# Output rows staged in eight row buffers, and one half block sent from the ACT queue

## The chip, the core and the metric

The kernel runs on one core of a Trainium2 chip. A core has five engines that run their own instruction streams: TensorE (PE, matrix products into PSUM), VectorE (DVE), ScalarE (ACT), GpSimd (POOL) and SyncE (SP, which here issues all DMA transfers). They are kept in order by semaphores: an instruction can wait until a counter has reached a value, and can raise one when it is done; a DMA raises its counter when its data has landed. The metric is the device time of one execution in microseconds, lower being better.

## The reference, cut to what matters

```python
x = A_x                                              # (1, 2048, 512) bf16
h = x + _A_ref(_layernorm(x, axis=-1), A_mem0, A_Wq, A_Wk, A_Wv, A_Wo, A_seg_len)
h2 = h + _B_ref(_layernorm(h, axis=-1), B_w_in, B_w_sp, B_b_sp, B_w_out)

def _B_ref(x, w_in, w_sp, b_sp, w_out):
    Fh = w_in.shape[-1] // 2                         # 896
    z = _gelu(jnp.einsum('bsd,df->bsf', x, w_in))
    z1 = z[..., :Fh].copy()
    z2 = _layernorm(z[..., Fh:], axis=-1)
    g = jnp.einsum('ts,bsf->btf', w_sp, z2) + b_sp[None, :, None]
    return jnp.einsum('bsf,fd->bsd', z1 * g, w_out)
```

`_A_ref` is an attention with 32 heads over 64 segments of 32 rows, one after the other, since each hands 8 memory rows to the next. `_B_ref` is a gated mixer over all 2048 rows. The change touches the last step of all: the product `(z1 * g) @ w_out`, the addition of `h`, and the way of the result to memory.

## The kernel before, in words

The 2048 rows are held as 16 row blocks of 128 rows, one row per partition. The first stage runs the 64 segments; it ends near 688 us. In it `part` (line 232) is a ring of eight row buffers of 128 x 512 values: the ACT engine writes segment s's attention output into buffer `s % 8` (`part_evac`, line 671), and PE reads it in `mem_out` (line 675) and `F_group` (line 692). The last of these reads belongs to row block 15 and is made at the start of the second stage. `xn` (line 234) is a pair of row buffers for normalised input.

The second stage computes `z2` and `z1T`, then, in four blocks `tb` of 512 rows, the mixing product (`mix`, line 1091: 16 matmuls per group) and its gate on DVE (`gate`, line 1096: two DVE instructions). As rows become complete, `out_mm` (line 1164) multiplies a row block with `w_out` (7 matmuls into one PSUM bank), and `out_done` (line 1170) adds `h` from `h_sb` on DVE into a row buffer and lets SP issue the DMA to the output. The first 12 output blocks are spread between the mixing groups of the following `tb`. The last four are written out by hand in lines 1202 to 1212: the first six matmuls of blocks 12 and 13, then, after the last gate, the seventh matmul of each with its `out_done`; then block 14 whole; then block 15 as two halves of 256 columns, in banks 5 and 7.

The instruction order of each engine is the order in which the program adds operations. The waits are worked out from tokens: `Emitter.add` (line 53) makes an operation wait for the last writer of each token that it reads, and for the last writer and all readers of each token that it writes; `finalize` (line 110) drops a wait that an earlier one of the same engine implies. The DMA out of a row buffer is a reader of that buffer's token. With two buffers, `xn[:, rb % 2]`, the addition of block rb therefore waits until the DMA of block rb - 2 has landed:

```python
tok = [("xo_out", rb % 2, hf) for hf in range(2) if d0 <= 256 * hf < d1]
dve(... out=xn[:, rb % 2, d0:d1] ..., writes=tok + [("xn", rb % 2)] * (rb < 2))
sp(lambda e: e.dma_start(outr[:, rb, d0:d1], xn[:, rb % 2, d0:d1]), reads=tok)
```

After its own stream each engine runs `run` (line 1893): it loads a flag from memory (line 1896; the flag says whether a slower general path is needed), and branches over that path (line 1900) to the end of the block (line 1905), where it drains and reports. SP first waits for the landing of the last DMA of every one of its DMA semaphores (line 1899). When all have reported, GpSimd releases them, and the program ends. ACT and GpSimd have no work in the last output blocks: they wait for the flag (line 1215), written at 795.8 us, and go to the end then.

Of the kernel before, what the change touches and what calls it, by code (L numbers as in the profile page):

```python
# [10 lines left out]
ALU = mybir.AluOpType  # L11
# [158 lines left out]
def fast_path(nc, st, keep, A_x, A_mem0, A_Wq, A_Wk, A_Wv, A_Wo, A_seg_len, B_w_in, B_w_sp, B_b_sp, B_w_out, out):  # L170
    S = A_x.shape[1]
    D = A_x.shape[2]
# [6 lines left out]
    RB = S // 128  # L179
# [16 lines left out]
    em = Emitter(n_dma_sems=40)  # L196

    def sb(name, shape, dt):
        return st.enter_context(nc.sbuf_tensor("f_" + name, shape, dt))
# [5 lines left out]
    def region(off, n):  # L205
        return arena[:, off:off + n]
# [25 lines left out]
    part = sb("part", [128, 8, 512], BF)  # L232
    partx = sb("partx", [128, 512], BF)
    xn = sb("xn", [128, 2, 512], BF)
# [28 lines left out]
    ps = st.enter_context(nc.psum_tensor("f_ps", [128, 8, 512], F32))  # L263
# [5 lines left out]
    def PB(b):  # L269
        return ("ps", b)  # L270

    def sp(fn, **k):
        return em.add("sp", fn, dma=True, **k)
# [15 lines left out]
    def dve(fn, **k):  # L289
        return em.add("dve", fn, **k)  # L290
# [552 lines left out]
    h_sb = region(RB * 512, RB * D).rearrange("p (rb d) -> p rb d", rb=RB)  # L843
# [14 lines left out]
    for s in range(NSEG):  # L858
        j4 = s % 4
        rb = s // 4  # L860
# [244 lines left out]
    def zbank():  # L1105
        zcnt[0] += 1
        return 5 + zcnt[0] % 3
# [5 lines left out]
    for rb in range(RB):  # L1113
# [19 lines left out]
        if rb in (2, 3):  # L1133
            r, j, bank = RB - 4 + rb, (rb - 1) % 2, zbank()
# [27 lines left out]
    outr = out[0].rearrange("(rb p) d -> p rb d", p=128)  # L1162

    def out_mm(rb, fbs, bank, d0=0, d1=D):
        for fb in fbs:
            pe(lambda e, fb=fb: e.matmul(ps[:, bank, 0:d1 - d0], lhsT=z1T[:, fb, rb * 128:(rb + 1) * 128], rhs=w_out[:, fb, d0:d1],  # L1166
                                         start=(fb == 0), stop=(fb == FB - 1)),
               reads=["w_out", ("z1T", fb, rb // 4)], writes=[PB(bank)])

    def out_done(rb, bank, d0=0, d1=D):  # L1170
        tok = [("xo_out", rb % 2, hf) for hf in range(2) if d0 <= 256 * hf < d1]
        dve(lambda e: e.tensor_tensor(out=xn[:, rb % 2, d0:d1], in0=ps[:, bank, 0:d1 - d0], in1=h_sb[:, rb, d0:d1], op=ALU.add),
            reads=[PB(bank), ("hs", rb)], writes=tok + [("xn", rb % 2)] * (rb < 2))
        sp(lambda e: e.dma_start(outr[:, rb, d0:d1], xn[:, rb % 2, d0:d1]), reads=tok)

    def out_rb(rb):
        bank = 2 + rb % 2
        out_mm(rb, range(FB), bank)
        out_done(rb, bank)
# [4 lines left out]
    for tb in range(NTB):  # L1184
        for fb in range(len(ACC) if tb == 0 else 0, FB):
            if tb == 0:
                bank = 5 + fb % 3
            else:
                bank = MB[mcnt % 3]
# [14 lines left out]
    for rb in pend[:2]:  # L1204
        out_mm(rb, (FB - 1,), 2 + rb % 2)
        out_done(rb, 2 + rb % 2)
    out_mm(RB - 2, range(FB), 6)
    out_done(RB - 2, 6)
    for d0 in (0, 256):
        bank = 7 if d0 else 5  # L1210
        out_mm(RB - 1, range(FB), bank, d0, d0 + 256)
        out_done(RB - 1, bank, d0, d0 + 256)

    for eng in Emitter.ENGS:
        em.add(eng, None, reads=["flag"])
# [668 lines left out]
def build_kernel(nc, A_x, A_mem0, A_Wq, A_Wk, A_Wv, A_Wo, A_seg_len, B_x, B_w_in, B_w_sp, B_b_sp, B_w_out, out):  # L1884
    args = (A_x, A_mem0, A_Wq, A_Wk, A_Wv, A_Wo, A_seg_len, B_w_in, B_w_sp, B_b_sp, B_w_out, out)
    with contextlib.ExitStack() as keep:
        with contextlib.ExitStack() as st:
            em, sems, dsems, flag = fast_path(nc, st, keep, *args)
# [88 lines left out]
```

The softmax here doesn't subtract the row's maximum and nothing guards it: scores larger than these inputs give would overflow.

## Time and profile before

| | |
|---|---|
| time, median of 6 runs | 870.91 us (869.59 to 871.8) |
| time of the profiled execution | 870.33 us |
| its span, first to last instruction | 868.5 us |
| PE busy | 847.5 us, 98% of the span |
| DVE / ACT / POOL busy | 502.0 / 467.0 / 157.9 us |
| granted TensorE clock, mean | 0.997 |
| last matmul starts | 860.66 us |
| output DMAs (line 1174) | 15 of 128 KB, 2 of 64 KB, all from SP |

The page splits the span by engine in 40 slices of 21.7 us, follows the chain of work that ended last, and groups instructions by line. A time line shows instructions in order with the idle time before them in brackets and what ended it. Lines that begin with an engine and a "q" (DVEq, SPq) belong to the engine's sequencer: waits, branches, loads of a flag, DMA issues. The duration of a DMA issue is the time that the issuing queue spends on it, not the time of the transfer; the landing is marked apart, by the semaphore that the DMA raises. The difference between the profiled execution's time and its span, 1.8 us, lies around the first and the last instruction.

### The profile page before, as it was taken

To read this page: it belongs to the slowest core of one execution; us is meant where nothing else is said; L and a number is where in the kernel's file an instruction comes from. 1 tells how busy PE (TensorE), PEld (TensorE's weight loads), DVE (VectorE), ACT (ScalarE), POOL (GpSimd) and SP (SyncE) were. 2 spreads that over 40 slices of the span, in tenths; PEclk is the share of its full clock that TensorE was granted. 3 is DMA by queue.
4 is the path that set the end of the run, shared out by engine and by line. 5 is a ranking of instruction groups with operands and counts; after the bars stand their busy time and mean duration, and the time that the engine had idled before them with its cause. 6 is when DMAs were issued, how large, how long until landed. Compare 5 with 4: busy or idle time off the path is not lost.

```text
span 868.5 us, 45456 instructions
## 1 busy us (share of the span) xinstructions
PE 847.5 (98%) x22453; PEld 432.3 (50%) x18876; DVE 502.0 (58%) x1246; ACT 467.0 (54%) x1291; POOL 157.9 (18%) x427
## 2 busy tenths in 40 slices
PE   6999999999999999999999999999999999999996
PEld 6664545544545444554444544545444444444443
DVE  3446666666666666666666666566565554454343
ACT  3445666666666666666666666666666655300000
POOL 1712112121122112121212112121111122100000
PEclk9999999999999999999999999999999999999998
DMA  9972332213141232222250313322221880033001
GB/s 320 380 221 70 71 70 74 65 39 84 33 86 40 68 64 30 73 68 63 67 97 26 83 51 81 80 70 71 47 68 43 197 267 1 0 109 111 25 19 33
DMA packets 114183, 75.23 MB, mean 87 GB/s; under 512 B 70712, under 2 KB 99520, under 8 KB 113984
## 3 DMA queue, kind: packets, MB, share of 16 engines
q1 hardware_dynamic: 113984, 72.26, 30.5%
q8 instruction: 164, 2.69, 1.3%
q14 instruction: 35, 0.29, 0.1%
HBM read 39.46 MB, written 20.58 MB: 69 GB/s over the span
## 4 chain that ended last, share of the span: by engine, by line
PE 96%; DVE 2%; DMA 1%; issue 1%; ACT 0%; POOL 0%; SPq 0%; DVEq 0%
PE f_ps L280 30%; PE f_ps L660 13%; PE f_ps L281 13%; PE f_ps L1092 11%; PE f_ps L710 3%; PE f_ps L426 3%; PE f_ps L461 3%; PE f_ps L1054 3%; PE f_ps L574 3%; PE f_ps L1085 3%; PE f_ps L625 3%; PE f_ps L1166 2%; PE f_ps L631 1%; PE f_ps L554 1%; PE f_ps L681 1%
## 5 line engine op out<-in xcount | busy, mean ns | idle before, releaser
L280 PE MATMUL f_ps<-f_arena,f_hT 128*32 128x512 bf16 (+1 forms) x5120 | 352.3, 337 | 1.6 <-issue 0.5
L281 PE MATMUL f_ps<-f_arena,f_hT 128*32 128x256 bf16 (+1 forms) x3072 | 214.3, 308 | 0.0
L280 PEld LDWEIGHTS f_ps<-f_arena,f_hT 128*32 128x32 bf16 x5120 | 120.8, 96 | 168.5 <-issue 85.6
L518 ACT ACTIVATE f_Tst<-f_ps 128x512 bf16<-128x512 f32 (+1 forms) x320 | 149.9, 510 | 57.5 <-PE f_ps L280 53.8
L660 PE MATMUL f_ps<-f_arena,f_cT 128*32 128x256 bf16 x4096 | 133.9, 273 | 1.2 <-ACT f_cT L645 1.1
L597 POOL TENSOR_TENSOR f_E_sb<-f_R_sb,f_E_sb 128x64 bf16<-128x64 f32 x128 | 48.0, 375 | 378.4 <-ACT f_R_sb L589 378.4
L526 DVE STREAM_TRANSPOSE f_QT<-f_Tst 128x256 uint32<-128x256 uint32 x128 | 57.1, 446 | 94.6 <-ACT f_Tst L518 94.6
L660 PEld LDWEIGHTS f_ps<-f_arena,f_cT 128*32 128x32 bf16 x4096 | 92.4, 95 | 35.1 <-ACT f_cT L645 21.4
L1092 PE MATMUL f_ps<-f_arena 128*128 128x512 bf16 x448 | 100.6, 379 | 0.0
L617 DVE TENSOR_SCALAR f_V_sb<-f_ps 128x512 bf16<-128x512 f32 (+1 forms) x128 | 70.6, 551 | 41.0 <-PE f_ps L280 41.0
L672 ACT ACTIVATE f_part<-f_ps 128x256 bf16<-128x256 f32 x128 | 49.1, 383 | 67.2 <-PE f_ps L660 67.2
L647 DVE TENSOR_SCALAR f_cT<-f_ps 128x160 bf16<-128x160 f32 (+1 forms) x192 | 61.0, 374 | 38.6 <-PE f_ps L631 38.6
L645 ACT ACTIVATE f_cT<-f_ps 128x160 bf16<-128x160 f32 (+1 forms) x192 | 53.0, 349 | 39.7 <-PE f_ps L631 39.7
L1092 PEld LDWEIGHTS f_ps<-f_arena 128*128 128x128 bf16 x448 | 43.7, 98 | 52.8
L526 DVE STREAM_TRANSPOSE f_KT<-f_Tst 128x128 uint32<-128x128 uint32 (+1 forms) x192 | 66.1, 356 | 2.8
L585 ACT ACTIVATE f_R_sb<-f_ps 128x160 f32<-128x160 f32 x128 | 38.9, 304 | 33.7 <-PE f_ps L281 33.7
L1098 DVE TENSOR_TENSOR f_arena<-f_ps,f_arena 128x512 f32<-128x512 f32 x28 | 19.3, 690 | 54.4 <-PE f_ps L1092 52.4
L567 ACT ACTIVATE f_E_sb<-f_ps 128x224 bf16<-128x224 f32 x128 | 45.9, 358 | 0.0
L593 DVE TENSOR_TENSOR f_E_sb<-f_R_sb,f_E_sb 128x160 bf16<-128x160 f32 x128 | 44.6, 348 | 0.0
L589 ACT ACTIVATE f_R_sb<-f_R_sb 128x160 f32<-128x160 f32 x128 | 42.5, 332 | 2.0
L710 PE MATMUL f_ps<-f_arena,f_cTx 128*32 128x512 bf16 x512 | 40.5, 380 | 0.0
L280 PE MATMUL f_ps<-f_arena,f_hTe 128*32 128x512 bf16 x512 | 39.1, 382 | 0.0
(105 smaller groups left out, 1022.5 us busy)
## 6 DMA issues: line engine op xcount, KB each, us to landing
wT_d<-f_wst SPq DMA_DIRECT2D x32, 256.0 KB, 2.0
f_arena<-wT_d SPq DMA_DIRECT2D x32, 256.0 KB, 4.7
f_arena<-in_A_Wq_dram SPq DMA_DIRECT2D x4, 1024.0 KB
f_arena<-in_A_Wv_dram SPq DMA_DIRECT2D x4, 1024.0 KB
f_arena<-in_A_Wk_dram SPq DMA_DIRECT2D x4, 1024.0 KB, 15.5
f_arena<-in_A_Wo_dram SPq DMA_DIRECT2D x4, 1024.0 KB
f_Vx<-vext_d SPq DMA_DIRECT2D x128, 32.0 KB
f_xn<-in_A_x_dram SPq DMA_DIRECT2D x16, 128.0 KB, 3.1
```

Source lines behind the costliest of these rows:

```text
L280: return e.matmul(out, lhsT=lhsT, rhs=rhs, start=start, stop=stop, skip_group_check=True, tile_position=pos)
L281: return e.add_instruction(mybir.InstMatmult(name=nc.get_next_instruction_name(), engine=mybir.EngineType.PE, ins=[e.lower_ap(rhs), e.lowe ...
L518: act(lambda e: e.activation(out=st_.rearrange("p (hp i r) -> p hp i r", i=32, r=2), in_=ps[:, bank, 0:64 * np_].rearrange("p (hp r i) -> ...
L526: dve(lambda e: e.transpose(out=dst, in_=src), reads=tok, writes=[(nm, b, k) for k in halves(b, p0, np_)])
L597: pool(lambda e: e.tensor_tensor(out=ev, in0=rv, in1=ev, op=ALU.mult), reads=[("R", b), ("Ex", b)], writes=[("Ex", b)])
L617: dve(lambda e: e.tensor_scalar(out=dst, in0=src, scalar1=VSC, scalar2=None, op0=ALU.mult), reads=[PB(bank)], writes=tok)
L645: act(lambda e: e.activation(out=dst, in_=src, func=ACT.Copy, scale=UNSC), reads=[PB(PVB[c])], writes=tok)
L647: dve(lambda e: e.tensor_scalar(out=dst, in0=src, scalar1=UNSC, scalar2=None, op0=ALU.mult), reads=[PB(PVB[c])], writes=tok)
L660: pe(lambda e, h=h, g=g, i=i, b=b, c=c: e.matmul(ps[32 * g:32 * g + 32, bank, 0:d1 - d0], lhsT=cTh[:, i, 8:40], rhs=w_o[:, h, d0:d1], star ...
L672: act(lambda e: e.activation(out=part[:, s % 8, d0:d1], in_=ps[:, bank, 0:d1 - d0], func=ACT.Copy), reads=[PB(bank)], writes=[("part", s % ...
L710: pe(lambda e, h=h, g=g, i=8 * qr + bg: e.matmul(ps[32 * g:32 * g + 32, WXB, :], lhsT=cTx[:, rb % 2, i, :], rhs=w_o[:, h, :], start=(i < 4 ...
L1092: pe(lambda e: e.matmul(ps[:, bank, 0:TB], lhsT=z2[:, sc, fb * 128:(fb + 1) * 128], rhs=wTb[tb % 2][:, :, sc, :], start=(sc == 0), stop=(s ...
```

## The change

The output rows go to `part[:, rb % 8]` in place of `xn[:, rb % 2]`, with the tokens of `part`. The addition of block rb thus writes over what the DMA of block rb - 8 read, or, for blocks 0 to 7, over what the first stage left there. `out_done` gets an argument for the queue. All DMAs stay on SP but that of the first half of block 15, which ACT issues. The buffers, their number and the arithmetic are unchanged.

```diff
-    def out_done(rb, bank, d0=0, d1=D):
-        tok = [("xo_out", rb % 2, hf) for hf in range(2) if d0 <= 256 * hf < d1]
-        dve(lambda e: e.tensor_tensor(out=xn[:, rb % 2, d0:d1], in0=ps[:, bank, 0:d1 - d0], in1=h_sb[:, rb, d0:d1], op=ALU.add),
-            reads=[PB(bank), ("hs", rb)], writes=tok + [("xn", rb % 2)] * (rb < 2))
-        sp(lambda e: e.dma_start(outr[:, rb, d0:d1], xn[:, rb % 2, d0:d1]), reads=tok)
+    def out_done(rb, bank, d0=0, d1=D, q="sp"):
+        tok = [("part", rb % 8, hf) for hf in range(2) if d0 <= 256 * hf < d1]
+        dve(lambda e: e.tensor_tensor(out=part[:, rb % 8, d0:d1], in0=ps[:, bank, 0:d1 - d0], in1=h_sb[:, rb, d0:d1], op=ALU.add),
+            reads=[PB(bank), ("hs", rb)], writes=tok)
+        em.add(q, lambda e: e.dma_start(outr[:, rb, d0:d1], part[:, rb % 8, d0:d1]), reads=tok, dma=True)
...
     for d0 in (0, 256):
         bank = 7 if d0 else 5
         out_mm(RB - 1, range(FB), bank, d0, d0 + 256)
-        out_done(RB - 1, bank, d0, d0 + 256)
+        out_done(RB - 1, bank, d0, d0 + 256, "sp" if d0 else "act")
```

## The prediction, made before the changed kernel ran

> **What bounds the kernel now.** I read the chain of waits first, then the time line of its last 12 us, then how each engine reaches the end of the program. The page's shares of the chain:
>
> ```profile
> PE 96%; DVE 2%; DMA 1%; issue 1%; ACT 0%; POOL 0%; SPq 0%; DVEq 0%
> ```
>
> PE carries 96%, and the change takes nothing from it. Only the 1% of DMA and the end can move. The chain from 855 us on (start, duration, what):
>
> ```profile
> 854.92 2.77 PE f_ps L1166 x12
> 857.69 0.02 issue
> 857.72 0.70 DVE f_xn L1172
> 858.42 0.02 issue
> 858.43 0.58 DMA out_dram<-f_xn
> 859.01 0.02 issue
> 859.03 3.91 DMA out_dram<-f_xn
> 862.94 0.04 DVEq L158
> 862.97 0.04 issue
> 863.02 0.42 DVE f_xn L1172
> ```
>
> PE leaves this chain at 857.69 though it works until 860.93: the last additions do not wait for PE, but for the DMA of block 13, issued at 859.03 and landed at 862.94. The time line of the same stretch, DVE's lines and SP's:
>
> ```profile
> 857.72 1.29 DVE L1172 TENSOR_TENSOR f_xn<-f_ps,f_arena 128x512 bf16<-128x512 f32 x2 [1.39 <-PE f_ps L1166]
> 858.43 7.40 SPq L1174 DMA_DIRECT2D out_dram<-f_xn  x5
> 860.19 0.69 DVE L1172 TENSOR_TENSOR f_xn<-f_ps,f_arena 128x512 bf16<-128x512 f32 x1 [1.18 <-PE f_ps L1166]
> 863.02 0.76 DVE L1172 TENSOR_TENSOR f_xn<-f_ps,f_arena 128x256 bf16<-128x256 f32 x2 [2.14 <-DMA out_dram<-f_xn]
> ```
>
> The wait of 1.18 us at 860.19 is put down to PE, but the trace's semaphore record shows PE done with block 14 at 859.42 and with the halves of block 15 at 860.18 and 860.95; block 12's DMA landed at 860.11. So this addition too waited for a DMA, some 0.75 us. All earlier additions (every 5 us in the blocks before, landing in 2.7 us in the median) start with PE: between 800 and 856 us no line of DVE names a DMA. The change gains at the very end or nowhere.
>
> After the last addition (ends 863.77) nothing is busy, and the span goes on for 4.8 us. From the listing of lines 1905 and 1896 (start of the only record at the right):
>
> ```profile
> L1905 ACTq DRAIN  x1: 66/66/66, 800.1 to 800.1; - x1
> L1905 PEldq DRAIN  x1: 73/73/73, 863.2 to 863.2; - x1
> L1905 DVEq DRAIN  x1: 58/58/58, 866.8 to 866.8; - x1
> L1905 SPq DRAIN  x1: 13/13/13, 868.3 to 868.3; - x1
> L1896 ACTq TENSOR_LOAD <-f_flag x1: 472/472/472, 796.0 to 796.0; - x1
> L1896 DVEq TENSOR_LOAD <-f_flag x1: 545/545/545, 863.1 to 863.1; - x1
> L1896 SPq TENSOR_LOAD <-f_flag x1: 531/531/531, 865.9 to 865.9; - x1
> ```
>
> SP reports last. Its issues of the halves start at 863.47 (0.33 us) and 863.84; the second takes 1.99 us where 0.33 is the median of line 1174, and ends at 865.83. Then come the flag, the walk over the DMA semaphores (line 1899, 866.45 to 867.97) and the branch. The walk meets the last half's semaphore at 867.04, just after its landing at 867.03; the rest to the end is 1.49 us.
>
> **The change part by part.** No instruction is added or removed on PE or DVE: 17 additions and 17 issues stay, one issue moves from SP to ACT.
>
> *Staging.* Block rb now waits for the DMA of rb - 8, which was issued over 40 us earlier, so the condition is always met; for blocks 0 to 7 the last PE reads of `part` lie at 688 us (line 695), 84 us before the first output addition at 772.7. For the first 12 blocks that is worth nothing, as they did not wait. At the end, with DVE starting 0.02 us behind PE's semaphore, as block 12 did (857.69 to 857.72):
> - block 14: 859.44 in place of 860.19, ends 860.13 (0.69 us);
> - first half of 15: 860.21 in place of 863.02, ends 860.63 (0.42 us);
> - second half: 860.97 in place of 863.36, ends 861.38 (0.41 us) in place of 863.77.
>
> So the last output is in its buffer 2.39 us earlier. What is late next is PE's last matmul itself.
>
> *SP's end.* Its issues follow the additions by about 0.02 us: block 14 at 860.16, the second half at 861.40. Two costs of that last issue are open. The issue lies between 0.33 us (median of its line) and 1.99 (its own row). Landing took 1.67 us from issue to mark for block 12, 3.1 and 3.2 for the halves, 3.9 for block 13. The slow ones lie beside fetches of instruction code: the DMA records show 16 KB blocks on queue 8 at 860.10 (1.65 us) and 863.91 (1.55 us), each on one DMA engine; block 13's last sixteenth landed 1.19 us after the first of them ended, the others at 860.7. PE's stream does not change, so the fetch of 860.10 to 861.75 remains. On its engine block 13's share lands at 862.94, block 14's by its own row 0.3 later, the halves perhaps 0.2 each: an estimate of 863.6 for the last. I take this, 2.2 us after issue; then SP ends at 863.6 + 1.49 = 865.1. With the shortest landing it is 863.07 + 1.49 = 864.6, with the 3.2 of its own row 866.1. An issue held for 1.99 us shifts SP as a whole by 861.40 - 863.84 = -2.44, to 866.1.
>
> *DVE's end.* From flag load to drain it took 866.83 - 863.08 = 3.75 us; the load follows the dispatch of the last addition, so 861.03 + 3.75 = 864.8, and 0.2 us for the release (868.32 to 868.53): 865.0.
>
> *The half on ACT.* ACT waits for DVE's 860.63; behind the wait are its flag load, branch and drain, which before were done at 800.2, 68 us ahead of need. That cover goes. ACT has issued no DMA in this trace. Nearest row: SP's half block, 0.33 us; SP's very first issue took 0.69 where the shortest of its group took 0.46, so I add 0.23: 0.56 us. Bounds: 0.33, and 1.99 of the held row; below nothing it cannot go, as ACT issued none. From flag load to the end of the drain ACT took 800.21 - 795.96 = 4.25 us. Sum: 860.65 + 0.56 + 0.04 + 4.25 + 0.21 = **865.7**; with the bounds 865.5 and 867.2.
>
> Here two rules of the Trainium skill stand against rows. "Advanced Engine Details and Errata", section Control Flow Timing, gives a compare-and-branch about 108 ns. The records of the branch agree (45 ns on ACT, 72 on DVE), but the drain behind it starts 3.6 us later on ACT and 3.1 on DVE. By the rule ACT would be done near 862.1 and SP's 865.1 would end the span, 3.4 us early; by the row ACT ends it at 865.7. I take the row.
>
> "DMA: Bandwidth & Descriptors", section Issuing engines are not separate DMA queues, says that DMAs from several engines share the same DMA engines, and that a second issuer saves only the sequencer's issue time. The row: the second half's issue, 0.38 us behind the first, was held for 1.66 us more than the median. If the first half's issue caused that, ACT's queue saves 1.66; by the rule it saves at most 0.33, and with staging alone the issues would lie 0.75 us apart (860.65 and 861.40), so nothing. I take the rule: the move to ACT is worth nothing on SP, and by the sum costs 0.6 us (865.7 against 865.1).
>
> *Sum.* 868.53 - 865.7 = 2.8 us. In the profiled run 870.33 - 2.8 = 867.5, with the 1.8 us around the span unchanged. That run lies 0.6 us under the median; from the median, 870.91 - 2.8 = **868.1 us**.
>
> **The rivals.**
> 1. *The end only shifts.* The last issue is held again for 1.99 us: 866.1, a gain of 2.4, so 868.5 us. For it: its own row. Against: the fetch that began just behind that issue (863.91) follows PE's drain (863.24) and will not meet an issue at 861.40; block 14's issue at 860.91, inside the other fetch, took 0.33.
> 2. *ACT becomes the bound with a held issue.* 1.99 us on ACT: 867.2, a gain of 1.4, so 869.5 us, within what can be told from no change. For it: its issue at 860.65 lies inside the code fetch. Against: the 0.33 of block 14 in the same place.
> 3. *ACT so late that it is slower.* If ACT's stream must fetch code before the DMA (2.0 us, the time from ACT's branch to its fetch at 798.5) and the first issue takes as long as the longest on SP (3.99 us, a weight load at 21.8), then 860.65 + 2.0 + 3.99 + 0.04 + 4.25 + 0.21 = 871.1, 2.6 us later than before: 873.5 us. It is slower from an ACT delay of 3.4 us on. For it: nothing shows ACT's queue. Against: all output rows on SP but one take 0.33.
> 4. *The change does not do what it says*: another wait of block 14 or 15 remains (for `h_sb`, or for reads of `part`), and the time stays at 870.9. All of these are tens of us old.
>
> **How the numbers follow.** The forecast (ends between 864.6 and 866.1) 0.60, rival 1 0.12, rival 2 0.14, rival 3 0.10, rival 4 0.04. A difference under 0.2%, 1.74 us, cannot be told from none in this kernel. Faster by more: forecast and rival 1, 0.72; same: rivals 2 and 4, 0.18; slower 0.10. The range goes from a gain of 3.9 us (867.0) to rival 2 (869.5), each widened by some 0.5 us, as single runs lie up to 1.3 us from their median: 866.5 to 869.9.
>
> **What would show it.** No DVE line after 857 names a DMA; additions start at about 859.4, 860.2 and 861.0; ACT's flag load near 861.3 and its drain near 865.4, last or within half a us of SP's. Wrong if the additions keep their gaps, if PE's last matmul moves, if SP's last issue is again near 2 us, or if ACT's issue takes over 2 us.

## The result, and the profile after

The changed kernel takes 868.16 us (median of 19 runs, 866.49 to 869.74) against 870.68 us for the kernel before (39 runs, 868.86 to 872.34): ratio 0.997, 95% interval 0.9963 to 0.9976. The prediction was 868.1. The gain is small, but the interval excludes no change.

The profiled execution took 869.62 us, with a span of 867.8. Its time line from 859 us on, DVE's, SP's and ACT's lines, answers to the one shown of before:

```profile
859.80 1.29 DVE L1172 TENSOR_TENSOR f_part<-f_ps,f_arena 128x512 bf16<-128x512 f32 x2 [1.39 <-PE f_ps L1166]
860.52 3.65 SPq L1174 DMA_DIRECT2D out_dram<-f_part  x4
861.53 1.19 DVE L1172 TENSOR_TENSOR f_part<-f_ps,f_arena 128x512 bf16<-128x512 f32 x2 [0.44 <-PE f_ps L1166]
862.75 0.37 ACTq L1174 DMA_DIRECT2D out_dram<-f_part  x1
863.06 0.42 DVE L1172 TENSOR_TENSOR f_part<-f_ps,f_arena 128x256 bf16<-128x256 f32 x1 [0.34 <-PE f_ps L1166]
```

No line of DVE names a DMA any more. Block 14's addition starts 1.73 us after block 12's, before 2.47; the halves of block 15 start at 862.29 and 863.06, so 2.49 and 3.26 us after it, before 5.30 and 5.64. The clock has no part in this: in both profiles it is 1.00 up to 863 us, and the means (0.997 and 1.000) differ by what was granted after PE's last matmul (0.50 from 864 us on before, 0.95 changed). The chain of waits over the same stretch:

```profile
856.96 0.05 issue
857.01 6.02 PE f_ps L1166 x34
863.03 0.02 issue
863.06 0.42 DVE f_part L1172
```

PE now stays in it to its last matmul. What is late next shows in the listings of lines 1905 and 1896, and in the list of what SP waited for:

```profile
L1905 PEldq DRAIN  x1: 73/73/73, 865.2 to 865.2; - x1
L1905 ACTq DRAIN  x1: 67/67/67, 866.7 to 866.7; - x1
L1905 DVEq DRAIN  x1: 57/57/57, 866.7 to 866.7; - x1
L1905 SPq DRAIN  x1: 13/13/13, 867.6 to 867.6; - x1
L1896 ACTq TENSOR_LOAD <-f_flag x1: 487/487/487, 863.1 to 863.1; - x1
```
```profile
SPq L1899 <- DMA out_dram<-f_part: 1.0, 2, 0.8
```

SP is last again. Its walk over the DMA semaphores now waits for landings, 1.0 us in all: the last half (the second half of block 15) was issued at 863.51 and landed at 866.30, and 1.5 us of walk, branch and drain follow.

The two spans differ by only 0.7 us, since in this execution block 12's addition came 2.09 us later. Those 2 us arose in the first stage, which the change leaves alone: its last matmul of line 660 starts at 689.1 us, against 687.0. Over all profiles of this study block 12 starts between 857.2 and 860.6 us. I therefore count a **tail**, from the start of block 12's addition to the end of the span. Up to that point PE had the same work in every kernel. The tail was 868.53 - 857.72 = 10.81 us before and 867.81 - 859.80 = 8.01 us after: 2.80 us less.

### The profile page after: what moved, and what is told of

The parts are those of the page before. It is cut to its first block, busy times and chain, and to the rows that moved or that the text cites. A ratio compares the mean times of both kernels' runs of the same rounds, so it can differ in the third digit from the quotient of the medians.

```text
span 867.8 us, 45456 instructions
## 1 busy us (share of the span) xinstructions
PE 848.0 (98%) x22453; PEld 432.1 (50%) x18876; DVE 502.1 (58%) x1246; ACT 467.5 (54%) x1291; POOL 158.0 (18%) x427
## 4 chain that ended last, share of the span: by engine, by line
PE 96%; DVE 2%; issue 1%; DMA 1%; ACT 0%; SPq 0%
PE f_ps L280 30%; PE f_ps L660 13%; PE f_ps L281 13%; PE f_ps L1092 11%; PE f_ps L710 3%; PE f_ps L426 3%; PE f_ps L461 3%; PE f_ps L1166 3%; PE f_ps L1054 3%; PE f_ps L574 3%; PE f_ps L625 3%; PE f_ps L1085 3%; PE f_ps L631 1%; PE f_ps L554 1%; PE f_ps L681 1%
```

## The experiments

All times in the table are microseconds after the start of block 12's addition; "last landing" is the last half's. The ratio is that of the measured times to the kernel before on the same chip.

| kernel | addition 14 | first half of 15 | last landing | tail | ratio (95% interval) |
|---|---|---|---|---|---|
| before | 2.47 | 5.30 | 9.31 | 10.81 | |
| changed | 1.73 | 2.49 | 6.50 | 8.01 | 0.997 (0.9963 to 0.9976) |
| staging alone | 1.73 | 2.49 | 6.44 | 7.94 | 0.9977 (0.9966 to 0.9989) |
| ACT's queue alone | 2.47 | 5.30 | 8.76 | 10.27 | 1.0001 (0.9991 to 1.0011) |
| two blocks staged | 1.73 | 2.49 | 6.59 | 8.08 | 0.9974 (0.9963 to 0.9984) |
| before, PE held | 2.47 | 3.08 | 6.52 | 8.75 | 0.998 (0.9968 to 0.9993) |
| changed, short walk | 1.73 | 2.49 | 6.30 | 7.25 | 0.9971 (0.9962 to 0.998) |
| staging, short walk | 1.73 | 2.49 | 6.32 | 7.27 | 0.9977 (0.9967 to 0.9987) |
| changed, no branch | 1.73 | 2.49 | 5.23 | 6.62 | 0.9968 (0.9955 to 0.998) |
| before, no branch | 2.47 | 3.08 | 5.67 | 7.07 | 0.997 (0.9959 to 0.9981) |
| changed, PE held | 1.73 | 2.49 | 5.25 | 8.45 | 0.9976 (0.9967 to 0.9986) |
| changed, again | 1.73 | 2.49 | 5.52 | 7.32 | 0.9973 (0.9961 to 0.9984) |
| changed, short walk, again | 1.73 | 2.49 | 6.41 | 7.36 | 0.9954 (0.994 to 0.9967) |

A tail is that of one execution. The changed kernel gave 8.01 and 7.32, so differences under some 0.7 us between single tails are not shown by one pair.

The ratios place these kernels against the one before, but hardly against each other: the ten from 0.9968 to 0.998 have intervals that all contain 0.997. Four lie above the range that was expected for them: staging alone, the two with a short walk in their first runs, and the changed kernel without the branch. For the last, the tail shows 4.2 us saved and the time 2.8. So what a variant saves beyond the change itself is read from single tails, and the times do not settle it.

**The parts apart.** Staging alone: the changed kernel with

```diff
-        out_done(RB - 1, bank, d0, d0 + 256, "sp" if d0 else "act")
+        out_done(RB - 1, bank, d0, d0 + 256, "sp")
```

> The rows are staged in eight buffers as in the change, and both halves of block 15 leave by SP. The tail is counted from the start of block 12's addition to the end of the span: 10.81 us before, 8.01 us changed. Theory (the waits on the buffers carry the gain, ACT's queue is worth nothing on SP): tail 7.4 to 8.3 us, ratio to the kernel before 0.9960 to 0.9975, SP's issues of the halves 0.75 us apart. Rival (ACT's queue carries part of it, since the second issue of a pair is held up): the last issue near 2 us, tail 9.0 to 10.0 us, ratio 0.998 to 0.999.

The tail of 7.94 is the theory's. The rival saw something real, though: the first half's issue on SP took 1.07 us, and the second could start only 4.06 us after block 12, where it starts at 3.71 in the changed kernel. So the two issues lay 1.12 us apart, not 0.75. The last half landed no later for that (6.44 against 6.50).

ACT's queue alone: the kernel before with `out_done(RB - 1, ..., "sp" if d0 else "act")`, its rows in `xn`.

> Two row buffers as before, and ACT issues the first half of block 15. Theory: the additions keep their gaps (block 14 about 2.5 us and the first half about 5.3 us after block 12), ACT drains some 4 us after its issue, and the tail stays at 10.3 to 10.9 us, ratio 0.9993 to 1.0005. Rival (the issue held for 1.99 us was held by the half ahead of it in the same queue): SP's last issue 0.33 us and the tail 9.7 to 10.1 us, ratio 0.9988 to 0.9993.

The additions keep their gaps, in the time line of this kernel. The line below it lists all of SP's output issues (shortest, median and longest in ns):

```profile
862.98 0.69 DVE L1172 TENSOR_TENSOR f_xn<-f_ps,f_arena 128x512 bf16<-128x512 f32 x1 [1.18 <-PE f_ps L1166]
865.81 0.76 DVE L1172 TENSOR_TENSOR f_xn<-f_ps,f_arena 128x256 bf16<-128x256 f32 x2 [2.14 <-DMA out_dram<-f_xn]
866.27 0.37 ACTq L1174 DMA_DIRECT2D out_dram<-f_xn  x1
```
```profile
L1174 SPq DMA_DIRECT2D out_dram<-f_xn x16: 332/332/338, 776.2 to 866.6; - x16
```

SP's last issue took 0.33 us here, where it took 1.99 before, with a code fetch of PE beginning as close to it (at 866.69 beside 866.60). So in this pair of profiles the hold was gone with the first half out of SP's queue, as the rival had it. Of the 1.66 us the tail kept 0.54, because now the landing held up the walk, and the time did not move (1.0001). The tail of 10.27 lies just under the theory's range and above the rival's.

A neighbour in the queue is not all there is to a held issue. In the changed kernel the last issue on SP, 1.26 us behind block 14's, still took 0.66 us, and two halves back to back on SP took 0.43 to 0.45 where no fetch of PE was near (the two kernels below that have two buffers and no early fetch). In seven profiles one of SP's last output issues took over 0.5 us, and each ended 0.29 to 0.40 us after a 16 KB fetch of PE had ended. What holds the issue stays open.

Two blocks staged: eight buffers for blocks 14 and 15 alone, both halves by SP.

```diff
...
+        buf, name, i = (part, "part", rb % 8) if rb >= RB - 2 else (xn, "xo_out", rb % 2)
...
```

> Only blocks 14 and 15 are staged in other buffers; blocks 0 to 13 use the two buffers as before, and all DMAs leave by SP. Theory (before waited in the last two blocks alone): the same as with eight buffers and one queue, tail 7.4 to 8.3 us, ratio 0.9960 to 0.9975. Rival (the earlier twelve blocks also gained something): ratio over 0.998, block 12's addition later in the span than with eight buffers by more than the runs scatter.

The tail is 8.08 and the ratio 0.9974, as with eight buffers: the first 14 blocks need no other buffers. As far as these runs can tell, all that the change is worth lies in two waits, that of block 14 and that of the first half of block 15.

**Why the wait was long.** Before, block 13's DMA landed 3.9 us after its issue, block 12's after 1.67. An output DMA raises its semaphore in sixteen steps, one for each sixteenth of its data. I call a step a mark and the data behind it a share; the DMA has landed when the sixteenth mark is there. After its branch PE fetches 16 KB of instruction code, which stands in the DMA records as one block of 16 KB on queue 8 (before, 1.05 us behind the start of the branch). In all nine profiles in which PE is not held and the branch is there, fifteen of block 13's marks come within 1.7 us, and the last one 1.1 to 1.2 us after the fetch ends: the fetch ends at 861.75 and the mark comes at 862.94 before, 863.76 and 864.96 changed, 862.29 and 863.48 with staging alone.

The records of single DMA packets show the queue. Before, 248 of the 256 packets (1 KB each) of blocks 12 and 13 have started by 860.4. The other eight, one share, start at 861.74, when the fetch ends, and run one behind the other to 862.45; eight of block 14 follow in the same way to 862.80. To move the fetch, I ran the kernel before with

```diff
+    em.add("pe", None, after=[em.by_eng["dve"][-1]])
     for eng in Emitter.ENGS:
         em.add(eng, None, reads=["flag"])
```

> The kernel before, with PE made to wait for DVE's last addition ahead of its flag load and branch, so that PE's fetch of instruction code comes after the output DMAs of blocks 12 to 14. Theory (that fetch, 16 KB on one DMA engine, is what made block 13's DMA land 3.9 us after its issue): it lands within 1.6 to 2.0 us, the first half's addition starts 3.0 to 3.4 us after block 12's in place of 5.3, and the tail is 8.5 to 9.5 us, ratio 0.9975 to 0.9990. Rival (landing is slow for another reason): it stays over 3.5 us, and the tail is 10.8 us or more, ratio 1.000 or above.

Its chain of waits and the drains:

```profile
862.72 0.55 DVE f_xn L1172
863.27 0.06 issue
863.33 0.41 DVE f_xn L1172
863.75 0.32 DVEq L1897
864.06 0.01 DVE f_xn L1172
```
```profile
L1906 SPq DRAIN  x1: 13/13/13, 868.0 to 868.0; - x1
L1906 PEldq DRAIN  x1: 73/73/73, 868.7 to 868.7; - x1
```

Block 13 landed in 1.67 us, the first half follows block 14's addition by 0.61 us, as closely as block 13's follows block 12's, and a wait *added* to PE made the kernel before faster: ratio 0.998, interval 0.9968 to 0.9993. The long wait on block 13's DMA is gone from the chain. The short one is still there, though the view puts it down to PE as it did before: block 14's addition starts 2.47 us after block 12's, not 1.73, since it waits for block 12's landing at 862.64. The price stands in the second view: PE, whose branch now starts later, drains last.

The same was done from the other side: both kernels without the general path, that is without the flag load, the branch and the code behind it (of lines 1895 to 1903 SP's walk stays; the fast path, which computes the output here, is whole).

```diff
-            r = e.alloc_register("flag_" + name)
-            e.reg_load(r, flag[:])
...
-            with e.If(e.snap(r) != 0):
...
-                gem.emit(name, e, gsems, gdsems)
```

> The changed kernel without the general path: no flag load, no branch and no code behind it, so no engine fetches code from beyond a branch at the end. Theory (code fetches slow the last landings): all output DMAs land within 1.6 to 2.0 us, tail 6.0 to 6.6 us in place of 8.01, ratio to the kernel before 0.9940 to 0.9960. Rival (landings of 2.8 us have another cause): they stay over 2.4 us, tail 7.0 us or more.

> The kernel before without the general path. Theory (the two row buffers cost so much only because a code fetch delays block 13's landing): it lands within 2.0 us, the first half's addition starts 3.0 to 3.4 us after block 12's, and this kernel lies only 0.2 to 0.6 us behind the changed one without the general path, tail 6.2 to 7.0 us. Rival (two buffers cost 2.8 us of themselves): it lies 2 us or more behind it.

All landings fell to 1.5 to 1.7 us, and the tails to 6.62 and 7.07 (each 0.1 us or less above the range). The two kernels lie 0.45 us apart, where with the fetch it was 2.8. Even of the 0.45 the buffers make only 0.15, by which the last addition is later: these two kernels differ in the queue as well, and with both halves on SP the second was issued another 0.18 us later and took 0.12 us more to land. In the measured time the kernel before without the branch stands where the changed kernel does (0.997 both). The time lines of the last additions, first without, then with two buffers and no branch:

```profile
861.41 1.19 DVE L1172 TENSOR_TENSOR f_part<-f_ps,f_arena 128x512 bf16<-128x512 f32 x2 [0.44 <-PE f_ps L1166]
862.94 0.42 DVE L1172 TENSOR_TENSOR f_part<-f_ps,f_arena 128x256 bf16<-128x256 f32 x1 [0.34 <-PE f_ps L1166]
```
```profile
861.82 1.35 DVE L1172 TENSOR_TENSOR f_xn<-f_ps,f_arena 128x512 bf16<-128x512 f32 x3 [1.18 <-PE f_ps L1166]
```

In the second, three additions run back to back, since block 14's waited for block 12's landing at 861.74; block 13 landed at 862.34 and delayed nothing, for the first half could follow at 862.43 at the earliest.

**What ends the changed kernel.** SP's walk goes over all DMA semaphores, two to an instruction but for the first; half of the 18 instructions come after the last half's semaphore. With the walk cut to what SP's earlier waits do not imply:

```diff
         done = em.final_dma_ops()
+        known = em.by_eng["sp"][-1].clock
+        rest = [d for d in done if known.get(("dma", d.dma_sem), -1) < d.dma_val]
...
-                for d in done:
+                for d in rest:
                     e.wait_ge(dsems[d.dma_sem], d.dma_val)
```

> The changed kernel, with SP's last walk cut to the DMA semaphores that its earlier waits do not already imply. Theory (in the changed kernel the landing of the last half ends the span, and half of SP's 18 waits come after it for nothing): the last wait ends with that landing, 6.5 us after block 12's addition, the end follows 0.6 to 0.8 us behind or with the drains of DVE and ACT, tail 7.0 to 7.6 us in place of 8.01, ratio to the kernel before 0.9955 to 0.9970. Rival (ACT's late branch ends the span or comes to end it): ACT drains last and the tail stays at 7.6 us or more.

> Eight buffers, both halves by SP, and the short walk. Theory (ACT's queue is worth nothing): tail 6.9 to 7.5 us, within 0.3 us of the same with ACT's queue, ratio 0.9955 to 0.9970. Rival (two queues help once the walk is off the path): tail over 0.3 us longer than with ACT's queue.

The listing of the waits and of the drains, short walk with ACT's queue:

```profile
L1901 SPq EVENT_SEMAPHORE  x4: 27/28/28, 863.1 to 864.3; - x4
```
```profile
L1907 ACTq DRAIN  x1: 67/67/67, 864.5 to 864.5; - x1
L1907 DVEq DRAIN  x1: 58/58/58, 864.8 to 864.8; - x1
L1907 SPq DRAIN  x1: 53/53/53, 865.0 to 865.0; - x1
```

There are four waits in place of 18, and DVE and SP drain within 0.2 us of each other. Both tails, 7.25 and 7.27, are some 0.7 us under their counterparts. ACT's queue makes no difference that the runs can tell, and ACT drains last in none of the kernels.

> The changed kernel with PE held until DVE's last addition. Theory: all output DMAs of blocks 12 to 14 land within 2.0 us, but PE's code fetch and branch (about 4 us) now start 3.9 us after block 12's addition, so PE drains last near 8.0 us and the tail is 8.0 to 8.4 us: the late landing is traded for a late PE, and nothing is gained over the changed kernel. Rival (the late landing is all that counts): tail 7.0 to 7.6 us.

With PE held in the changed kernel every landing took 1.5 to 1.7 us, and the tail is 8.45 all the same, just over the theory's range, because PE drains last:

```profile
L1906 SPq DRAIN  x1: 13/13/13, 865.8 to 865.8; - x1
L1906 DVEq DRAIN  x1: 57/57/57, 866.1 to 866.1; - x1
L1906 PEldq DRAIN  x1: 73/73/73, 867.4 to 867.4; - x1
```

The last landing alone thus does not set the end: PE's fetch and branch must be run through somewhere.

The changed kernel and its short walk were then run once more, side by side:

> The changed kernel itself, beside its version with the short walk on the same chip. Theory: tail 7.8 to 8.2 us, ratio to the kernel before 0.996 to 0.998.

> The changed kernel with the short walk of SP. Theory: tail 7.1 to 7.4 us, 0.7 us less than the changed kernel, so a median 0.4 to 1.0 us below it. Rival (what the span saves is not seen in the time): a median within 0.2 us of it or above.

The changed kernel's second tail, 7.32, missed its range. PE's code fetch was 1.20 us long in place of 1.63, SP's last issue took 0.33 us in place of 0.66, and the last half landed 5.52 us after block 12, not 6.50. SP then drained at 864.0, and DVE was last at 864.3:

```profile
L1905 SPq DRAIN  x1: 13/13/13, 864.0 to 864.0; - x1
L1905 DVEq DRAIN  x1: 57/57/57, 864.3 to 864.3; - x1
```

The packet records say why the last half was late in the first profile. Its share behind PE's fetch landed at 865.65, 5.85 us after block 12. Its last two shares started only at 865.39 and landed at 866.28 and 866.30: two code fetches of 8 KB had run from 864.75 and 864.98 to 865.39 and 865.40. They began 1.0 and 1.3 us behind the branches of DVE and ACT (both at 863.7). In the second profile these fetches began at 862.32, after the half's last packet (862.22), and the share behind PE's fetch was the last. With staging and both halves on SP only one such fetch is in the way, since ACT has branched long before, and one share is late. So ACT's queue lets the last half be issued 0.35 us earlier and then puts a second fetch in its way. This order is read from the records; no run moved the 8 KB fetches alone.

So the walk is the bound only when the last half lands late: the short walk's second tail, 7.36, is no shorter than this one. In this set of runs the short walk's median was 867.73 us and the changed kernel's 868.39, but the intervals of the ratios overlap. Whether the short walk beats the change stays open; that it beats the kernel before is shown twice (0.9971 and 0.9954).

## Why the prediction was right, point by point

*The bound and the additions.* Right to 0.01 us. Against block 12 the additions were put at 1.72, 2.49 and 3.25 us; they came at 1.73, 2.49 and 3.26. The wait put down to PE at 860.19 had been a DMA's, and the staged kernels show it gone. That the first 12 blocks gain nothing is shown by staging two blocks alone.

*SP's end.* The mis-sized term is the landing: 2.2 us from issue to landing was taken for the last half, and the two profiles of the changed kernel gave 2.79 and 1.81. The queue behind PE's fetch was worked out rightly: the last half's share in it was put at 863.6, which is 5.9 us after block 12, and landed at 5.85 in the first profile and, behind a shorter fetch, at 5.52 in the second. The sum left out the 8 KB fetches behind the branches of DVE and ACT, which held two other shares until 6.50 in the first. SP's drain came 7.78 us after block 12 there, where 7.2 was the sum, and at 6.80 in the second. The bounds, 1.67 and 3.2, held both.

*DVE's end.* The drain was put at 7.1 us after block 12, and measured at 6.95 and 7.04. It was the last in the second profile.

*The half on ACT.* This step failed in its conclusion. The forecast had ACT end the span, 0.6 us behind SP. Its issue took 0.37 us, not 0.56, and flag load to drain 866.74 - 863.15 = 3.59 us, not 4.25; so ACT drained at 6.87 us and 6.70 us after block 12 in place of 7.7, which is 0.9 us and 0.1 us ahead of SP. The row that the 4.25 came from lies at 796 us, in the middle of the `wT` loads; at the end of the program few transfers are in the way. That is an explanation, not shown by a run. Between the first rule that was weighed and its row, the row was the right choice: ACT's drain starts 2.9 us after its branch (863.73 to 866.67), shorter than the 3.6 of the row. (ACT's upper bound adds up to 867.1, not 867.2; nothing rests on the difference.)

*ACT's queue.* The sum took it as worth nothing on SP, by the second rule that was weighed. The time agrees: ACT's queue alone gives 1.0001, and with staging the tails are 7.94 and 8.01, or 7.27 and 7.25. The reason did not hold in full. With staging alone the first half's issue was held for 1.07 us, so that ACT's queue did free 0.35 us of SP's time, which was lost again at the landing. And in the one pair that tests it, the issue held for 1.99 us did depend on the half ahead in the same queue, which the sum had left as an "if"; of the time so freed most ended at a landing too.

*The total.* A gain of 2.8 us was forecast; the tails of the first pair of profiles give 2.80, the second profile of the changed kernel 3.49, and the medians of the times 2.5. That the first agrees so closely is luck: ACT's end was put 0.8 us too late, and SP's 0.6 us too early, so that SP ended where ACT had been expected. The mechanism of the gain, the end of the two waits, was right.

*What the prediction did not see.* It named the code fetch beside the slow landings, but treated the buffers as the cause of the wait. The runs show two causes that act together, the two buffers and PE's fetch holding back one share of a DMA, and most of the wait goes when either is taken away. Moving the fetch by a wait of PE alone took 2.06 us off the tail.

## What to carry to other kernels

A wait on a buffer here cost as much as the slowest of sixteen shares of the DMA before it, so ask what else is being transferred at that moment: here it was the instruction code of an engine that had just finished. Read the end of a program engine by engine, to its last drain. In the changed kernel the last two ends lay 0.8 us apart in one profile and 0.2 in the other, so a gain in one is soon capped by the next. A gain of 2 to 3 us in 870 can be read from a stretch of the trace with fixed work in front of it, where the spans themselves scatter by as much.

## What the runs showed that I had not expected

- A 16 KB fetch of instruction code held back one sixteenth of an output DMA: it landed 1.2 us after the fetch ended, 2.2 us after the other fifteen shares (862.94 against 860.70).
- Moving an issue to ACT moved ACT's branch to the end of the program, and with it one more 8 KB fetch, which another share of the last half had to wait for.
- A wait added to an engine that had nothing left to do shortened the program by 0.2% (0.998), by moving that fetch.
- A DMA issue on SP right behind another one lasted 1.99 us beside a fetch, and 0.33 us with the one ahead of it sent from ACT; without a fetch it lasted 0.45.
